# Attention into a gated feed-forward layer: x's sums on DVE, the gates in two pairs, an earlier w_out unit, and x's first parts in halves

## The chip, the cores and the metric

One core of a Trainium2 chip runs the whole program. Its engines work side by side, each through its own instructions in order: TensorE (PE, matmuls; PEld, its weight loads), VectorE (DVE), ScalarE (ACT), GpSimd (POOL), and SyncE (SP), which here only issues DMAs. The metric is the time of one execution on the device, in microseconds.

## What is computed

Attention with a causal mask and a decay made from f, for 8 batches, 8 heads, 576 positions and 64 columns a head; its output, as a matrix x of 4608 tokens by 512, goes through a feed-forward layer of width 2048:

```python
scores = scale * np.matmul(q, k.transpose(0, 1, 3, 2))
decay = cum[:, :, :, None] - cum[:, :, None, :]      # cum: running sum of log f
scores = np.where(causal, -1000000000.0, scores + decay)
attn = softmax(scores)
x = (attn @ v) as [4608, 512]
h = x @ w_in                                          # [4608, 2048]
sp = np.maximum(h, 0.0) + np.log1p(np.exp(-np.abs(h)))
g = h * erf(sp)
out = g @ w_out                                       # [4608, 512]
```

## The kernel before, in words

**Attention** is a loop over t = 0 to 68, two iterations to a pair of heads. Iteration t makes the scores of t and runs the later steps of t - 1 to t - 5 (exps, normalize, transposes, evacuate, values, store), so that all engines work at once. Between them lie jobs of the next stage: one or two weight jobs an iteration from `todo`, and `start_x`, which loads and splits x for the first visit of the feed-forward layer, at t = 44, 46, 48, 50, 52 and 59 to 63.

**The feed-forward layer** multiplies numbers split in two parts: a rounded high part and a remainder, three matmuls for a product. The 4608 tokens are six pairs of blocks of 384 tokens. A *visit* is one such pair with one half of the width 2048; there are 12 visits (v), the first six with the first half. A visit has four *units* (k = 0 to 3, `HU` = 4), each with 256 columns of the width, so there are 48 units (n). A unit makes, by a scheme of seven products instead of eight (`PRODUCTS`, sums and differences of the blocks of x and w_in), four tiles h of 128 x 384.

`step(n)` interleaves three units by hand: the products of unit n (`product`, line 169, 42 matmuls), the gates of unit n - 1, and the multiplication with w_out of unit n - 2 (`down`, line 230, 36 matmuls "y"). It has seven places i = 0 to 6; at each there is a product, then its reader, then other work, then six y matmuls (none at i = 5). The engines' order is the order in which step() writes the instructions.
- `consume`: the readers of the products. ACT copies products 0 and 2 (sa, line 182; h, line 187); DVE adds up the others (sb line 185, sc line 190, h line 193). Two PSUM banks alternate, so that a product can start only when its bank's last reader is done.
- Gates of unit n - 1: softplus (line 197) and erf (line 200) on ACT, each with its table load; `gate`, e times h, on DVE (line 203), four at i = 1; `halve` splits the result: a cast on ACT (gh, line 212) and a remainder on POOL (gl, line 213), four at i = 2.
- x of the next visit: five tiles t of 128 x 768 are loaded, and from them seven tiles x are made. `x_sum` (lines 107, 109, in the unit k = 2) and `late_sum` (line 129) make sums and differences; `split_x` casts (line 116), `rest_x` subtracts (line 121). `next_x` does this in the visit's last unit, k = 3, and `both_x` of x's tile 3 is in the next visit's first unit. Of a visit's eleven sums and remainders POOL does ten and DVE one; of the seven casts DVE does four and ACT three. Product i reads the x tile `XSLOT[i]` = 0, 5, 1, 4, 6, 2, 3.
- Weights come as 64-bit numbers. A piece is converted by `magnitude` (ACT, line 380), `normal`, `low_bits` (two instructions) and `join` (DVE, lines 383, 388, 390, 395), and split by `parts` (cast line 406, remainder on POOL line 407); pieces of w_in also need sums (line 433). In attention the first half of w_in and unit 0's w_out are made (`early_work`). `late_work` lays the rest into steps 2 to 20 (`moe.work[n, place]`): first w_out for units 1 to 3, which those units wait for, then the second half of all weights, one piece a step, whose parts (lhi, llo) go to DRAM through four buffers of one tag, and are read back from visit 5 on.

Steps 0 and 1 are already laid into attention's last iterations (`moe_products`, t = 64 to 67).

Of the kernel before, what the change touches and what calls it, by code (L numbers as in the profile page):

```python
# [11 lines left out]
F32 = mybir.dt.float32  # L12
# [4 lines left out]
ALU = mybir.AluOpType  # L17
# [5 lines left out]
P = 128  # L23
# [33 lines left out]
NU = FF // (2 * P)  # L57
HU = NU // 2
# [14 lines left out]
class Moe:  # L73
# [27 lines left out]
            src = self.xt_d[2 * half * P:2 * (half + 1) * P, at:at + TB]  # L101
            self.nc.sync.dma_start(out=t[j], in_=src.rearrange("(k p) t -> p k t", p=P))

    def x_sum(self, v, j):
        t, sub = self.t[v], self.nc.gpsimd
        if j == 0:
            sub.tensor_tensor(out=t[4], in0=t[2], in1=t[3], op=ALU.add)
        else:
            sub.tensor_tensor(out=t[2], in0=t[0], in1=t[2], op=ALU.subtract)

    def split_x(self, v, r, cast):

        t = self.t[v]
        x = self.x_tile(v, r)
        self.src[r] = t[{0: 0, 5: 0, 1: 1, 4: 4, 6: 2, 2: 1, 3: 3}[r]]
        cast(out=x[:, 0], in_=self.src[r])  # L116

    def rest_x(self, v, r, eng):

        x = self.x[v, r]  # L120
        eng.tensor_tensor(out=x[:, 1], in0=self.src[r], in1=x[:, 0].bitcast(F32), op=ALU.subtract)  # L121

    def both_x(self, v, r, cast, eng):
        self.split_x(v, r, cast)
        self.rest_x(v, r, eng)

    def late_sum(self, v, j, eng):
        t = self.t[v]
        eng.tensor_tensor(out=t[j], in0=t[4 if j == 0 else 1], in1=t[0], op=ALU.subtract)  # L129
# [135 lines left out]
    def step(self, n):  # L265

        v, k = divmod(n, HU)
        up, gates = n < self.n, 1 <= n <= self.n
        downs = self.down(n - 2) if n >= 2 else iter(())
        after = v + 1 < len(self.visits) and n < self.n  # L270
        if n >= 2 and (n - 1) % HU == HU - 1 and self.visits[(n - 1) // HU][1]:
            for tb in range(4):
                self.want_part((n - 1) // HU, tb)
        if gates:
            self.softplus(n - 1, 0)
            self.softplus(n - 1, 1)
        if after and (n == 2 or v and k == 1):
            self.load_x(v + 1)
        for i in range(7):
            if up:  # L280
                self.product(n, i)
                self.consume(n, i)
            if up and v and k == 0 and i == 0:
                self.both_x(v, 3, self.nc.vector.tensor_copy, self.nc.gpsimd)
            if gates and i == 0:
                for q in (2, 3):
                    self.softplus(n - 1, q)
                for q in range(4):
                    self.erf(n - 1, q)
            if after and i < 2:  # L290
                self.next_x(v + 1, k, i)
            if gates and i == 1:
                for q in range(4):
                    self.gate(n - 1, q)
            if gates and i == 2:
                self.do(n, "abs")
            if up and i == (2 if gates else 5):
                self.nc.scalar.preload_act_table_set(SOFTPLUS)
            if gates and i == 2:
                for q in range(4):  # L300
                    self.halve(n - 1, q)
            if after and i >= 2:
                self.next_x(v + 1, k, i)
            for _ in range(YCUT[i + 1] - YCUT[i]):
                next(downs, None)
            self.do(n, i)
            yield
        for _ in downs:
            pass
        if self.reload:  # L310
            self.reload(n)
# [3 lines left out]
def attention_moe(ctx, tc, q2, k2, vp, f, w_in, w_out, out):  # L315
    nc = tc.nc
# [153 lines left out]

    def late_work():

        pieces = [(a, i) for a in range(1, HU) for i in (2, 3)] + [(a, i) for a in range(HU, NU) for i in (2, 3, 0, 1)]
        load, magnitude, normal, low_bits, join, out_parts, quarter_parts, sums, sum_parts = weight_work(
            pieces, late_buf, nc.scalar.copy)
        for m in range(3):
            load(m)
        steps = {2: [0, 1, 2], 3: [3], 4: [4, 5]}
        steps.update({n: [n + 1] for n in range(5, len(pieces) - 1)})
        places = {1: [(3, 4, 5, 6)], 2: [(2, 3, 3, 4), (4, 5, 5, 6)], 3: [(2, 2, 3, 4), (3, 4, 4, 5), (5, 5, 6, 6)]}  # L480
        for n, ms in steps.items():
            for m, (a, b, c, d) in zip(ms, places[len(ms)]):
                moe.work[n, "abs"].append(lambda m=m: magnitude(m))
                moe.work[n, a].append(lambda m=m: normal(m))
                moe.work[n, b].append(lambda m=m: low_bits(m))
                moe.work[n, c].append(lambda m=m: (join(m), load({0: 3, 1: 4, 2: len(pieces)}.get(m, m + 2))))
                i = pieces[m][1]
                if m < 6:
                    moe.work[n, d].append(lambda m=m: out_parts(m))
                elif i >= 2:  # L490
                    moe.work[n + 1, 3].append(lambda m=m: out_parts(m))
                elif i == 0:
                    moe.work[n + 1, 3].append(lambda m=m: quarter_parts(m, 0))
                else:
                    moe.work[n + 1, 1].append(lambda m=m: sums(m, 0))
                    moe.work[n + 1, 2].append(lambda m=m: sums(m, 1))
                    for f in range(2):
                        moe.work[n + 1, 3 + f].append(lambda m=m, f=f: quarter_parts(m, f))
                    for w, at in enumerate((4, 5, 5, 6)):
                        moe.work[n + 1, at].append(lambda m=m, w=w: sum_parts(m, w))  # L500

    load_weight, todo = early_work()

    def start_x(j):

        if j == 0:
            a = wp.tile([P, 2, 2, TB], F32, name="ta", tag="wo2")
            b = wp.tile([P, 2, 2, TB], F32, name="tb", tag="wo3")
            c = wp.tile([P, 2, TB], F32, name="tc", tag="wo1")
            moe.t[0] = t = [a[:, 0], a[:, 1], b[:, 0], b[:, 1], c]  # L510
            for m, (token, half) in enumerate([(0, 0), (0, 1), (1, 0), (1, 1)]):
                for kd in range(2):
                    nc.sync.dma_start(out=t[m][:, kd], in_=moe.x_block(0, token, 2 * half + kd))
        elif j < 3:
            moe.x_sum(0, j - 1)
        else:
            r = [0, 5, 1, 4, 6, 2, 3][j - 3]
            moe.both_x(0, r, nc.scalar.copy, nc.vector if r in (0, 5) else nc.gpsimd)
            if r in (0, 1):
                moe.late_sum(0, r, nc.vector)  # L520

    moe_pools = ctx.enter_context(ExitStack())
    with ExitStack() as ph:
# [160 lines left out]
        NH = B * H  # L684
# [34 lines left out]
        for t in range(NH + 5):  # L719
# [52 lines left out]
        assert not todo and not pts and not held and not vals  # L772
# [54 lines left out]
```

## Time and profile before

| | us |
|---|---|
| median of 3 runs | 1158.06 (1157.95 to 1159.73) |
| the profiled execution | 1156.83 |
| its span, first to last instruction | 1155.0 |
| first product of unit 0 | 320.02 |
| last product's unit (47) starts | 1116.97 |

The mean clock that was granted to TensorE is 0.983 of full speed. In the rows of the profile, a group or a timeline row gives the line of the kernel, the engine, the operation, and output <- inputs by the program's tile names; in square brackets stands how long the engine was idle before it, and whose end released it. A row of the windows view gives a stretch, its length, then the busy time of PE, PEld, DVE, ACT and POOL with the number of instructions, the granted clock, and the share and rate of the DMA engines.

### The profile page before, as it was taken

The page shows a single profiled execution, that of the slowest core. Times are in us where ns is not written, and L with a number is a line of the kernel's source. Part 1 is how long each engine was busy: PE and PEld are TensorE (multiplying, and loading weights), DVE is VectorE, ACT ScalarE, POOL GpSimd, SP SyncE. Part 2 cuts the span into 40 slices and gives each one's busy share as a digit, 9 for nine tenths or more (in the row PEclk, how much of TensorE's full clock was granted, in tenths as well). Part 3 has the DMA queues.
Part 4 walks back from the last instruction along what each step waited for, and adds up shares of the span by engine and source line. Part 5 has one row for each costly group of instructions (what it writes and reads, how often), then busy time and mean ns, then how long its engine had stood idle before and what let it go on. Part 6 is the DMA issues. An engine that isn't in the chain of part 4 may idle for free.

```text
span 1155.0 us, 21292 instructions
## 1 busy us (share of the span) xinstructions
PE 1092.3 (95%) x7384; PEld 951.1 (82%) x7384; DVE 800.1 (69%) x1707; ACT 745.7 (65%) x1672; POOL 753.5 (65%) x841
## 2 busy tenths in 40 slices
PE   8999999999997799898998989999999999999997
PEld 7888888878886688787887878888888888888886
DVE  5898999999746666968778595645647484655632
ACT  3888888877865456575575666566655566555652
POOL 3787978798845836858576695755647383755612
PEclk8999999999999799999999999999999999999999
DMA  7777777776414032152433417542221313031022
GB/s 236 237 244 223 262 215 266 264 260 205 131 42 156 19 114 87 47 200 73 142 115 103 151 39 261 225 160 75 70 95 56 110 55 110 15 115 36 23 87 73
DMA packets 74907, 155.83 MB, mean 135 GB/s; under 512 B 7472, under 2 KB 27184, under 8 KB 73776
## 3 DMA queue, kind: packets, MB, share of 16 engines
q1 hardware_dynamic: 74800, 154.47, 40.1%
q8 instruction: 59, 0.97, 0.3%
q14 instruction: 48, 0.39, 0.1%
HBM read 114.44 MB, written 39.99 MB: 134 GB/s over the span
## 4 chain that ended last, share of the span: by engine, by line
PE 64%; POOL 12%; DVE 10%; ACT 6%; issue 4%; DMA 3%; SPq 0%; DVEq 0%; POOLq 0%; ACTq 0%
PE y L230 21%; PE m L169 20%; PE s L585 8%; PE o L666 8%; PE t L639 7%; POOL gl L213 4%; DVE e L203 3%; POOL x L121 3%; POOL t L129 3%; ACT e L200 2%; ACT e L197 2%; ACT L200 1%; DMA wi_d<-lhi 1%; DMA xt_d<-xo 1%; DVE ltop L395 1%
## 5 line engine op out<-in xcount | busy, mean ns | idle before, releaser
L169 PE MATMUL m<-x,wi 128*128 128x384 f32 x2016 | 404.7, 339 | 29.7 <-DVE sc L190 13.1
L169 PEld LDWEIGHTS m<-x,wi 128*128 128x128 f32 x2016 | 361.3, 190 | 63.0 <-DVE h L193 16.9
L230 PE MATMUL y<-wo,gh 128*128 128x512 f32 x1152 | 363.4, 396 | 16.0 <-POOL wo L407 12.4
L213 POOL TENSOR_TENSOR gl<-e,gh 128x384 fp32r<-128x384 f32 x192 | 221.5, 1183 | 236.4 <-ACT gh L212 209.5
L230 PEld LDWEIGHTS y<-wo,gh 128*128 128x128 f32 x1152 | 214.6, 190 | 46.8 <-POOL wo L407 14.1
L230 PE MATMUL y<-wo,gl 128*128 128x512 f32 x576 | 230.9, 401 | 0.0
L203 DVE TENSOR_TENSOR e<-e,h 128x384 f32<-128x384 f32 x192 | 185.9, 1028 | 33.1 <-ACT e L200 28.2
L627 POOL TENSOR_SCALAR pr<-pr,st 128x576 f32<-128x576 f32 (+4 forms) x320 | 164.0, 533 | 50.1 <-DVE st L623 26.0
L617 ACT ACTIVATE pr<-pr,st 128x576 f32<-128x576 f32 (+3 forms) x320 | 176.7, 557 | 8.0 <-DVE st L605 8.0
L121 POOL TENSOR_TENSOR x<-t,x 128x768 fp32r<-128x768 f32 x66 | 135.9, 2076 | 65.1 <-DVE x L116 65.1
L605 DVE CUSTOM_DVE_ANT_0 pr<-s,c 128x576 f32<-128x576 f32 (+3 forms) x320 | 136.5, 486 | 28.3 <-PE s L589 19.5
L197 ACT ACTIVATE e<-h 128x384 f32<-128x384 f32 x192 | 93.3, 520 | 82.4 <-DVE h L193 82.4
L230 PEld LDWEIGHTS y<-wo,gl 128*128 128x128 f32 x576 | 109.3, 190 | 23.0
L185 DVE TENSOR_TENSOR sb<-m,sa 128x384 f32<-128x384 f32 x48 | 26.7, 555 | 146.7 <-PE m L169 112.7
L585 PE MATMUL s<-k,q 64*128 64x320 f32 (+4 forms) x768 | 110.5, 410 | 3.4 <-DVE st L605 3.2
L648 ACT COPY pt<-t 128x512 f32<-128x512 f32 x128 | 73.9, 577 | 55.5 <-PE t L639 53.7
L212 ACT CAST gh<-e 128x384 fp32r<-128x384 f32 x192 | 88.9, 511 | 29.6 <-DVE e L203 28.7
L639 PE MATMUL t<-ident,pr 128*128 128x128 f32 x800 | 104.5, 276 | 3.0 <-ACT pt L648 2.9
L666 PE MATMUL o<-pt,v 128*64 128x128 f32 (+1 forms) x1920 | 103.1, 260 | 3.3 <-DVE xo L675 2.3
L666 PEld LDWEIGHTS o<-pt,v 128*64 128x64 f32 x1920 | 94.2, 138 | 13.4 <-DVE st L605 4.7
L639 PEld LDWEIGHTS t<-ident,pr 128*128 128x128 f32 x800 | 87.4, 141 | 15.2 <-issue 11.6
L585 PEld LDWEIGHTS s<-k,q 64*128 64x128 f32 x768 | 73.1, 188 | 32.1 <-issue 17.6
(96 smaller groups left out, 1206.2 us busy)
## 6 DMA issues: line engine op xcount, KB each, us to landing
v<-in_vp_dram SPq DMA_DIRECT2D x32, 576.0 KB, 6.9
c<-cum_d SPq DMA_DIRECT2D x62, 288.0 KB, 5.8
t<-xt_d SPq DMA_DIRECT2D x44, 384.0 KB, 5.5
q<-in_q_dram SPq DMA_DIRECT2D x32, 320.0 KB, 3.5
k<-in_k_dram SPq DMA_DIRECT2D x32, 288.0 KB, 3.9
xt_d<-xo SPq DMA_DIRECT2D x32, 288.0 KB, 6.2
part_d<-yo SPq DMA_DIRECT2D x36, 256.0 KB, 2.7
yo<-part_d SPq DMA_DIRECT2D x36, 256.0 KB, 3.0
```

The source lines that it names most:

```text
L121: eng.tensor_tensor(out=x[:, 1], in0=self.src[r], in1=x[:, 0].bitcast(F32), op=ALU.subtract)
L169: nc.tensor.matmul(out=ps, lhsT=w[:, wp, ws], rhs=x[:, xp, kd], start=first and kd == 0 and j == 0, stop=kd == 1 and j == 2 and i in (1, 2 ...
L197: self.nc.scalar.activation(out=e, in_=self.h[n, q], func=AF.Softplus)
L203: self.nc.vector.tensor_mul(self.e[n, q], self.e[n, q], self.h.pop((n, q)))
L213: nc.gpsimd.tensor_tensor(out=gl, in0=e, in1=gh.bitcast(F32), op=ALU.subtract)
L230: yield nc.tensor.matmul(out=y[tb], lhsT=g[:, cs], rhs=w[:, f, wp], start=first, stop=last)
L585: nc.tensor.matmul(out=s[j][:, at:at + k1 - k0], lhsT=q[h, PAD + START[i]:PAD + END[i]], rhs=k[h, k0:k1], start=i > 0, stop=i not in (0, 3))
L605: nc.vector.tensor_tensor_reduce(out=to[:, ::-1] if j else to, in0=score, in1=decay_, scale=-0.125, scalar=BIG, op0=ALU.add, op1=ALU.min, ...
L617: nc.scalar.activation(out=seg, in_=seg, func=AF.Exp, bias=st[:, 0, j, m:m + 1], scale=-1.0, accum_out=st[:, 1, j, m:m + 1])
L627: nc.gpsimd.tensor_scalar(out=seg, in0=seg, scalar1=st[:, 2, j, m:m + 1], scalar2=1.0, op0=ALU.mult, op1=ALU.mult)
L639: nc.tensor.transpose(out=b[:, n * P:(n + 1) * P], in_=probs[t][:, at:at + P], identity=ident)
L666: nc.tensor.matmul(out=o[h, to:to + width], lhsT=v[:, ch, h], rhs=pt[:, at[j]:at[j] + width], start=n == 0, stop=n == len(parts) - 1, skip ...
```

## The change

1. `x_sum`, `late_sum` and `rest_x` of all visits but the first run on DVE; `split_x` always casts on ACT. They are laid out anew: `next_x` does x0, x5, x1, x4 and the cast of x6 in the unit k = 3, and the new `last_x` does the rest of x6, x2 and x3 at i = 0, 1, 2 of the next visit's first unit.
2. Gates 0 and 1 stay at i = 1, gates 2 and 3 go to i = 3; halve of 0 and 1 stays at i = 2, of 2 and 3 goes to i = 3.
3. `late_work` starts one step earlier: unit 1's w_out is converted in step 1, in attention's tail, with buffers in the places of w_out 2 and 3; its parts come at i = 1 of step 2. Units 2 and 3 follow in steps 2 to 4. For the second half of the weights a visit's pieces are two of w_in in its unit k = 1, one of w_out in k = 2 and one in the next visit's k = 0, none in k = 3 (where the remaining parts of a w_out piece still come, at i = 2). The seven parts of w_in lie in k = 2.
4. x of the first visit is loaded from t = 24 on; its sums and its tiles 0 and 5 are made in halves of 384 columns, one job every second iteration up to t = 58. The other five tiles stay at t = 59 to 63.

```diff
-    def x_sum(self, v, j):
-        t, sub = self.t[v], self.nc.gpsimd
+    def x_sum(self, v, j, eng, kd=slice(0, 2)):
+        t = self.t[v]
...
     def next_x(self, v, k, i):
...
         if i == 1:
-            self.split_x(v, 0, dve)
-            self.rest_x(v, 0, pool)
-            self.late_sum(v, 0, pool)
+            self.split_x(v, 0)
+        elif i == 2:
+            self.rest_x(v, 0, dve)
+            self.late_sum(v, 0, dve)
+        elif i == 3:
+            self.split_x(v, 5)
+            self.split_x(v, 1)
         elif i == 4:
-            self.split_x(v, 5, dve)
-            self.both_x(v, 1, act, pool)
-            self.late_sum(v, 1, pool)
+            self.rest_x(v, 5, dve)
         elif i == 5:
-            self.rest_x(v, 5, self.nc.vector)
-            self.both_x(v, 6, act, pool)
+            self.rest_x(v, 1, dve)
+            self.late_sum(v, 1, dve)
+            self.split_x(v, 4)
         elif i == 6:
-            self.both_x(v, 4, dve, pool)
-            self.both_x(v, 2, act, pool)
+            self.rest_x(v, 4, dve)
+            self.split_x(v, 6)
+
+    def last_x(self, v, i):
+
+        dve = self.nc.vector
+        if i == 0:
+            self.split_x(v, 2)
+            self.rest_x(v, 6, dve)
+        elif i == 1:
+            self.rest_x(v, 2, dve)
+            self.split_x(v, 3)
+        elif i == 2:
+            self.rest_x(v, 3, dve)
...
             if up and v and k == 0 and i == 0:
-                self.both_x(v, 3, self.nc.vector.tensor_copy, self.nc.gpsimd)
+                self.last_x(v, 0)
...
-            if gates and i == 1:
-                for q in range(4):
+            if gates and i in (1, 3):
+                for q in (i - 1, i):
                     self.gate(n - 1, q)
+            if up and v and k == 0 and i in (1, 2):
+                self.last_x(v, i)
...
-            if gates and i == 2:
-                for q in range(4):
+            if gates and i in (2, 3):
+                for q in (2 * i - 4, 2 * i - 3):
                     self.halve(n - 1, q)
...
     def late_work():
 
-        pieces = [(a, i) for a in range(1, HU) for i in (2, 3)] + [(a, i) for a in range(HU, NU) for i in (2, 3, 0, 1)]
+        pieces = [(a, i) for a in range(1, HU) for i in (2, 3)] + [(a, i) for a in range(HU, NU) for i in range(4)]
...
+        first, second, only = (2, 2, 4), (4, 5, 6), (4, 5, 6)
+        plan = [(1, first, 2, 1), (1, second, 2, 1), (2, first, 3, 2), (2, second, 3, 3), (3, (5, 5, 6), 4, 2), (4, first, 4, 5)]
+        for n in range(5, 5 + HU * HU, HU):
+            plan += [(n, first, n + 1, 3), (n, second, n + 1, 3), (n + 1, only, n + 2, 2), (n + 3, only, n + 4, 2)]
+        for m, (n, (a, b, c), to, at) in enumerate(plan):
+            moe.work[n, "abs"].append(lambda m=m: magnitude(m))
+            moe.work[n, a].append(lambda m=m: normal(m))
+            moe.work[n, b].append(lambda m=m: low_bits(m))
+            moe.work[n, c].append(lambda m=m: (join(m), load(m + 2) if m > 1 else None))
+            i = pieces[m][1]
+            if i >= 2:
+                moe.work[to, at].append(lambda m=m: out_parts(m))
+            elif i == 0:
+                moe.work[to, at].append(lambda m=m: quarter_parts(m, 0))
+            else:
+                moe.work[to, 2].append(lambda m=m: (sums(m, 0), sums(m, 1)))
+                for f in range(2):
+                    moe.work[to, at + f].append(lambda m=m, f=f: quarter_parts(m, f))
+                for w in range(4):
+                    moe.work[to, at + (3 + w) // 2].append(lambda m=m, w=w: sum_parts(m, w))
...
+    def first_x():
+
+        work = [lambda j=j: load_first(j) for j in range(4)]
+        halves = [slice(kd, kd + 1) for kd in range(2)]
+        for j in range(2):
+            work += [lambda kd=kd, j=j: moe.x_sum(0, j, nc.gpsimd, kd) for kd in halves]
+        for r in (0, 5):
+            work += [lambda kd=kd, r=r: moe.split_x(0, r, kd) for kd in halves]
+            work += [lambda kd=kd, r=r: moe.rest_x(0, r, nc.vector, kd) for kd in halves]
+            if r == 0:
+                work += [lambda kd=kd: moe.late_sum(0, 0, nc.vector, kd) for kd in halves]
+        return work
...
-            if NH - 20 <= t < NH - 10 and t % 2 == 0:
-                start_x((t - NH + 20) // 2)
+            if t >= 24 and t % 2 == 0 and x_work:
+                x_work.pop(0)()
             if NH - 5 <= t < NH:
-                start_x(t - NH + 10)
+                start_x(t - NH + 5)
+            if t == NH:
+                load_late(0)
+                load_late(1)
```

More of the change, by code (lines that the diff above doesn't have):

```diff
@@ L102, in load_x, with split_x, rest_x, late_sum @@
             self.nc.sync.dma_start(out=t[j], in_=src.rearrange("(k p) t -> p k t", p=P))
-    def x_sum(self, v, j):
-        t, sub = self.t[v], self.nc.gpsimd
+    def x_sum(self, v, j, eng, kd=slice(0, 2)):
+        t = self.t[v]
         if j == 0:
-            sub.tensor_tensor(out=t[4], in0=t[2], in1=t[3], op=ALU.add)
+            eng.tensor_tensor(out=t[4][:, kd], in0=t[2][:, kd], in1=t[3][:, kd], op=ALU.add)
         else:
-            sub.tensor_tensor(out=t[2], in0=t[0], in1=t[2], op=ALU.subtract)
-    def split_x(self, v, r, cast):
+            eng.tensor_tensor(out=t[2][:, kd], in0=t[0][:, kd], in1=t[2][:, kd], op=ALU.subtract)
+    def split_x(self, v, r, kd=slice(0, 2)):
         t = self.t[v]
[L114 to L118, printed above, removed]
-        x = self.x[v, r]
[L121 to L127, printed above, removed]
+        if (v, r) not in self.x:
+            self.x_tile(v, r)
+            self.src[r] = t[{0: 0, 5: 0, 1: 1, 4: 4, 6: 2, 2: 1, 3: 3}[r]]
+        self.nc.scalar.copy(out=self.x[v, r][:, 0, kd], in_=self.src[r][:, kd])
+    def rest_x(self, v, r, eng, kd=slice(0, 2)):
+        x = self.x[v, r]
+        eng.tensor_tensor(out=x[:, 1, kd], in0=self.src[r][:, kd], in1=x[:, 0, kd].bitcast(F32), op=ALU.subtract)
+    def late_sum(self, v, j, eng, kd=slice(0, 2)):
         t = self.t[v]
-        eng.tensor_tensor(out=t[j], in0=t[4 if j == 0 else 1], in1=t[0], op=ALU.subtract)
+        eng.tensor_tensor(out=t[j][:, kd], in0=t[4 if j == 0 else 1][:, kd], in1=t[0][:, kd], op=ALU.subtract)
     def next_x(self, v, k, i):
-        act, dve, pool = self.nc.scalar.copy, self.nc.vector.tensor_copy, self.nc.gpsimd
+        dve = self.nc.vector
         if k == 2 and i in ((4, 5) if v == 1 else (0, 1)):
-            self.x_sum(v, i - (4 if v == 1 else 0))
+            self.x_sum(v, i - (4 if v == 1 else 0), dve)
         if k != HU - 1:
@@ L447, in late_buf @@
     def late_buf(kind, m, shape, dt=F32):
-        if kind == "raw" and m == 2:
-            kind = "tt"
+        if m < 2 and kind in ("raw", "top"):
+            if m == 0:
+                shared[kind] = wp.tile([P, 2, shape[1]], dt, name=f"tail_{kind}", tag={"raw": "wo3", "top": "wo2"}[kind])
+            return shared[kind][:, m]
         tag, bufs = {"raw": ("raw", 2), "top": ("top", 3), "tt": ("tt", 1), "hi": ("ws", 4), "lo": ("ws", 4)}[kind]
         return moe.eb.tile(shape, dt, name=f"l{kind}{m}", tag=tag, bufs=bufs)
+    shared = {}
     def early_work():
@@ L471, in late_work @@
     def late_work():
-        pieces = [(a, i) for a in range(1, HU) for i in (2, 3)] + [(a, i) for a in range(HU, NU) for i in (2, 3, 0, 1)]
+        pieces = [(a, i) for a in range(1, HU) for i in (2, 3)] + [(a, i) for a in range(HU, NU) for i in range(4)]
         load, magnitude, normal, low_bits, join, out_parts, quarter_parts, sums, sum_parts = weight_work(
             pieces, late_buf, nc.scalar.copy)
-        for m in range(3):
-            load(m)
-        steps = {2: [0, 1, 2], 3: [3], 4: [4, 5]}
@@ L479, in late_work @@
[L479 to L500, printed above, removed]
@@ L502, in attention_moe, with load_first @@
+        return load
     load_weight, todo = early_work()
-    def start_x(j):
+    load_late = late_work()
+    def load_first(j):
         if j == 0:
@@ L509, in start_x @@
             c = wp.tile([P, 2, TB], F32, name="tc", tag="wo1")
[L510 to L520, printed above, removed]
+            moe.t[0] = [a[:, 0], a[:, 1], b[:, 0], b[:, 1], c]
+        token, half = divmod(j, 2)
+        for kd in range(2):
+            nc.sync.dma_start(out=moe.t[0][j][:, kd], in_=moe.x_block(0, token, 2 * half + kd))
+    def first_x():
[9 more added lines that the diff above has]
+        return work
+    x_work = first_x()
+    def start_x(j):
+        r = [1, 4, 6, 2, 3][j]
+        moe.split_x(0, r)
+        moe.rest_x(0, r, nc.gpsimd)
+        if r == 1:
+            moe.late_sum(0, 1, nc.vector)
     moe_pools = ctx.enter_context(ExitStack())
@@ L771, in attention_moe @@
                 moe.ps_m = moe_pools.enter_context(tc.tile_pool(name="ps_m", bufs=1, space=PSUM, side="right"))
-        assert not todo and not pts and not held and not vals
+        assert not todo and not x_work and not pts and not held and not vals
     moe.eb = ctx.enter_context(tc.tile_pool(name="eb", bufs=1))
     moe.ps_y = ctx.enter_context(tc.tile_pool(name="ps_y", bufs=1, space=PSUM))
-    late_work()
+    load_late(2)
+    load_late(3)
     last = HU * NPAIR
```

1 line of the change is left out of this document (added).

## The prediction

> **What bounds the kernel now.** I read the page first, then cut the span into stages with the windows view, then asked who ended TensorE's waits in each stage (its timeline), then the costs of the instructions that the change moves.
>
> ```profile
> span 1155.0 us, 21292 instructions
> PE 1092.3 (95%) x7384; PEld 951.1 (82%) x7384; DVE 800.1 (69%) x1707; ACT 745.7 (65%) x1672; POOL 753.5 (65%) x841
> 436.87:452.51 15.64, 15.64 (x80) 14.07 (x79) 9.64 (x16) 9.92 (x18) 9.09 (x7) 1.00 0.27 85
> 366.51:436.87 70.36, 54.52 (x236) 46.68 (x234) 43.72 (x53) 35.35 (x64) 47.23 (x31) 0.85 0.19 66
> 452.51:469.38 16.87, 15.80 (x79) 13.87 (x77) 13.11 (x14) 10.65 (x18) 12.12 (x9) 1.00 0.19 68
> 469.38:744.53 275.15, 257.29 (x1248) 226.85 (x1249) 202.54 (x248) 176.24 (x327) 194.16 (x139) 0.99 0.38 133
> 744.53:808.63 64.10, 63.10 (x313) 56.09 (x312) 34.27 (x43) 39.31 (x70) 37.63 (x27) 1.00 0.37 141
> 808.63:1067.82 259.19, 251.37 (x1250) 224.56 (x1248) 154.70 (x189) 151.28 (x268) 150.57 (x105) 1.00 0.23 74
> 1067.82:1085.69 17.87, 15.90 (x79) 13.94 (x78) 14.07 (x13) 10.58 (x19) 15.44 (x10) 1.00 0.00 0
> ```
>
> TensorE is the bound, and a unit without a wait takes 15.64 us (third row: PE busy for all of it). So I count each stage as its excess over 15.64 us a unit; the cuts lie at the first product of a unit, every 42 matmuls of line 169.
> - Units 3 to 5 (366.51 on): 70.36 - 3 x 15.64 = 23.4 us, with the clock at 0.85.
> - Unit 7 and the four visits after it, which still split weights: 1.2 + (275.15 - 16 x 15.64 = 24.9) = 26.1 us.
> - Visit 6: 1.5 us. Visits 7 to 10: 259.19 - 250.24 = 8.95, 2.24 a visit; visit 11's first unit 2.23. Together 12.7 us.
>
> Attention before that has its own rate. The first two rows hold four of its iterations each (from t = 44 and t = 49), the third two near its end (t = 60, 61):
>
> ```profile
> 219.68:238.60 18.92, 18.92 (x226) 15.76 (x223) 17.09 (x68) 15.18 (x49) 14.80 (x26) 1.00 0.97 337
> 243.28:266.20 22.92, 20.44 (x226) 16.52 (x223) 22.62 (x71) 16.48 (x51) 20.38 (x35) 1.00 0.63 212
> 299.51:310.56 11.05, 9.96 (x115) 8.44 (x112) 7.78 (x33) 9.06 (x27) 8.93 (x13) 1.00 0.26 83
> ```
>
> Undisturbed it is 18.92 us. Where start_x casts and subtracts whole tiles it is 22.92: 4.0 us lost, with DVE busy for 22.62. The third row loses 11.05 - 18.92 / 2 = 1.6.
>
> What ends TensorE's waits:
>
> ```profile
> 372.28 0.80 PE L230 MATMUL y<-wo,gh 128*128 128x512 f32 x1 [4.33 <-POOL wo L407]
> 402.66 0.80 PE L230 MATMUL y<-wo,gh 128*128 128x512 f32 x1 [5.88 <-POOL wo L407]
> 511.01 1.31 PE L169 MATMUL m<-x,wi 128*128 128x384 f32 x6 [1.03 <-ACT sa L182]
> 543.50 1.33 PE L169 MATMUL m<-x,wi 128*128 128x384 f32 x6 [2.02 <-DVE h L193]
> 822.93 2.35 PE L169 MATMUL m<-x,wi 128*128 128x384 f32 x12 [1.95 <-DVE sc L190]
> 436.87 1.21 PE L169 MATMUL m<-x,wi 128*128 128x384 f32 x6
> 439.30 1.21 PE L169 MATMUL m<-x,wi 128*128 128x384 f32 x6
> ```
>
> In units 3 and 4 it is w_out's parts that come late. At a visit's start it is a PSUM bank whose reader on DVE (h, sc) is late. The last two rows give the pitch, 2.43 us from a product to the next; the second half of a bank's pair must be read within one or two of these. Why DVE is late:
>
> ```profile
> 846.64 1.96 DVE L203 TENSOR_TENSOR e<-e,h 128x384 f32<-128x384 f32 x4 [0.21 <-ACT e L200]
> 862.46 6.09 DVE L203 TENSOR_TENSOR e<-e,h 128x384 f32<-128x384 f32 x4
> 850.69 0.56 DVE L190 TENSOR_TENSOR sc<-m,sb 128x384 f32<-128x384 f32 x1 [2.08 <-PE m L169]
> 850.64 3.93 POOL L213 TENSOR_TENSOR gl<-e,gh 128x384 fp32r<-128x384 f32 x4 [7.95 <-ACT gh L212]
> L121 POOL TENSOR_TENSOR x<-t,x 128x768 fp32r<-128x768 f32 x66 | 135.9, 2076 | 65.1 <-DVE x L116 65.1
> L121 DVE TENSOR_TENSOR x<-t,x 128x768 fp32r<-128x768 f32 x11 | 24.8, 2252 | 0.0
> L129 DVE TENSOR_TENSOR ta<-ta 128x768 f32<-128x768 f32 x1 | 1.0, 957 | 2.6 <-POOL x L121 2.6
> L116 ACT CAST x<-t 128x768 fp32r<-128x768 f32 x33 | 26.5, 834 | 69.4 <-POOL t L129 69.3
> ```
>
> Four gates take 1.96 us in a unit where POOL is idle, 6.09 in a visit's last unit, where POOL subtracts x tiles. Two-input work on DVE and POOL takes turns: the same 768 columns cost DVE 0.96 us alone and 2.25 beside POOL.
>
> **The change part by part.** *Second half and visit 6 (12.7 us).* Before, POOL did ten of a visit's eleven sums and remainders at some 2 us each. Now DVE does all eleven, at 0.96 us if POOL rests, and hands its four casts to ACT at 0.83. In the last unit DVE then holds six sums (5.7 us), four gates (2.0) and five bank readers of 0.55 (2.7): 10.4 of 15.64. POOL holds only the four gl of 1.0. I laid it out by hand: gates 0 and 1 meet an idle POOL; gates 2 and 3 take turns with two gl and end near 11.5 us; h of product 4, behind them, ends near 12, and is wanted at 13.2. Casts of x5 and x1 follow on ACT until 13.6, so x5's subtraction ends near 14.4, h of product 5 at 14.9 (wanted at 15.6), two sums, h of product 6 at 17.1 (wanted at 18.1). In the next unit x2 is ready at 7 us (wanted at 12.2) and x3 at 8.1 (13.2). Nothing is late: -12.7 us. What hides the sums is the slack of some 0.7 to 1.2 us in each of these; if it is gone, about 0.8 us a visit comes back, -8 at worst.
>
> *Units 2 to 5 (23.4 us).* Unit 1's w_out is now split in units 1 and 2, units 2's and 3's one unit ahead of use, so both waits above go, and with them the clock:
>
> ```profile
> 370.86:381.10 10.24, 7.46 (x18) 5.87 (x19) 2.82 (x5) 5.70 (x11) 7.02 (x5) 0.50 0.00 1
> 544.94:548.35 3.41, 3.41 (x11) 2.95 (x10) 2.16 (x4) 3.38 (x6) 3.19 (x2) 0.50 0.19 77
> 358.23 0.69 DVE L383 SCALAR_TENSOR_TENSOR ltop<-ltop,lraw 128x512 f32<-128x512 f32 x1 [1.20 <-ACT ltop L380]
> 360.50 0.68 DVE L395 SCALAR_TENSOR_TENSOR ltop<-ltop,lraw 128x512 int32<-128x512 int32 x1
> L407 POOL TENSOR_TENSOR wo<-ltop,wo 128x512 fp32r<-128x512 f32 x6 | 8.2, 1373 | 2.0 <-ACT wo L406 2.0
> ```
>
> What is next late is DVE. A piece costs it some 2.5 us (first and last of four instructions). Unit 2 has two pieces and two sums (5.0 + 1.9) beside gates and readers (4.7) and POOL's four gl and two w_out remainders (6.7), which it must take turns with: about 0.9 us over. Unit 3 has one piece and six sums; h of product 6 stands behind two of them and the piece, 2 us too late, which unit 4 pays, with 0.4 more of its own; units 3 and 5 about 0.7 each. After: 0.9 + 0.7 + 2.4 + 0.7 = 4.7, so -18.7. Bounds after: 1 (all hidden) to 12 (half remains).
>
> The second row here is a clock row: a wait of 2.02 us at 543.5 is followed by 3.41 us at half clock. The Trainium skill (TensorE: Matmul & The Clock Gate, section Why this matters for your kernels) asks only that gaps stay under about 3 us; by it, gaps like those that I leave would cost no clock. Here the measurement differs, so up to 1.7 us may follow a gap of 2; I keep that in the upper bound.
>
> *Attention's tail.* Steps 0 and 1 run between attention's last pieces:
>
> ```profile
> 343.05 1.28 ACT L298 ACT_TABLE_LOAD   x1
> 344.34 1.75 ACT L212 CAST gh<-e 128x384 fp32r<-128x384 f32 x4
> 346.00 0.58 ACT L648 COPY pt<-t 128x512 f32<-128x512 f32 x1
> 346.26 0.68 DVE L646 COPY pt<-t 128x512 f32<-128x512 f32 x1
> 347.77 1.66 PE L666 MATMUL o<-pt,v 128*64 128x128 f32 x32
> ```
>
> Two magnitudes now stand ahead of the table load on ACT (1.2 us), and gates 2 and 3 with their casts stand ahead of the last pt copies on DVE and ACT. Gate 3, taking turns with two gl from 346.1, ends near 348.9, its cast at 349.4, pt near 350; the o matmuls wait for pt until then instead of 347.77. That is +2.3 us; bounds 0 (gates win their turns) and +3.5.
>
> *First x parts in halves.* The same instructions, spread over iterations 24 to 58: the 4.0 us go, but DVE, at 17.1 of 18.92 us already, gets six half-size steps of some 0.5 us, and POOL four of 1.0; I let 1.0 stay. -3.0, bounds -4 and 0. The 1.6 us near the end are untouched. x's loads may wait on SP for a store of the same rows, but q, k and c behind them are asked for two iterations ahead. The two new weight loads at t = 64 wait on SP for x's last remainder; only a store two iterations on stands behind them. Both at nothing; if that cover is gone, a late load shows as a gap of PE of one transfer.
>
> *First half (26.1 us).* The two w_in pieces of a unit now meet in the visit's third unit: seven parts instead of six. The row that decides:
>
> ```profile
> 509.35 0.41 ACT L406 CAST lhi<-ltt 128x256 fp32r<-128x256 f32 x1
> 510.50 0.46 ACT L182 COPY sa<-m 128x384 f32<-128x384 f32 x1
> L407 POOL TENSOR_TENSOR llo<-ltt,lhi 128x256 fp32r<-128x256 f32 x16 | 11.8, 735 | 12.5 <-DMA wi_d<-llo 7.9 <-ACT lhi L406 2.3 <-ACT e L197 2.2
> ```
>
> The sixth part is cast at 509.35, 4.4 us into the next unit (504.95), because parts go through four buffers and each waits for POOL and a store; sa stands behind it on ACT, and TensorE waits 1.03 (row at 511.01). A seventh part puts sa about 1 us later: 2.0 us of wait, and now in the visit's last unit. There ACT is then 5 us late with the erfs, the cast of x0 and the table, so gates 2 and 3 meet gl 0 and 1 and end at about 16.5: h of product 4 is 1.7 us late; x5's subtraction pushes h of product 5 another 0.7; small ones 0.5. 4.9 a visit, four visits 19.6. The second unit, with two w_in pieces on DVE, 0.6 in three visits; the piece in the first unit 0.2 in four. After: 22.2, so -3.9. Bounds: 3 after (the part chain ends before sa) to 34 (the turns go on into the next unit, with a half clock).
>
> Sum: -12.7 - 18.7 + 2.3 - 3.0 - 3.9 = -36.0. The profiled execution took 1156.83, so 1120.8; the median of the runs is 1.23 above it, and on that scale I forecast 1122.0 us.
>
> **The rivals.**
> 1. *The part chain is no trouble*: without the second unit's copies in between, its seventh part ends before sa is due. For it: six of the seven parts waited for POOL or a store, and the stores share SP with fewer others now. Against: the wait is there at six parts already. First half 4 instead of 22: 1104.
> 2. *w_out is in time, but units 2 to 4 stay bound by DVE*: x's sums and the pieces pile up, half of 18.7 comes back: 1131.
> 3. *Slower: DVE becomes the bound in a visit's last unit.* If each sum there costs the 2.25 us of the row for DVE beside POOL, and a gate 1.0, the unit needs 6 x 2.25 + 4 + 2.7 = 20.2, 4.6 too much, in eleven visits 51; with some 1.8 more in the first and the third unit of the four loaded visits (14) that is 65 for the 38.8 won: +26, and with -19.4 from the rest +7, 1165. It decides from a mean of about 2.1 us a sum. Against it: POOL's four gl hold 4 us a unit, so six sums can't wait over 0.7 each on average, 1.6 to 1.7 in all. The Trainium skill (SBUF — State Buffer, section Who interferes with whom) says of a DVE instruction with two SBUF inputs that it contends with POOL's reads, whole instructions at a time; by it too a sum waits for at most the gl in hand. Row 862.46 agrees.
>
> **How the numbers follow.** The forecast's own case, 1112 to 1130, gets 0.55; rival 1 0.27; rival 2 0.14; rival 3 0.04. A measurement of this kernel tells about 0.2% (2.3 us) from no change. Slower is rival 3, 0.04; same is the far end of rival 2, 0.02; faster 0.94. The range reaches down to rival 1's value and up past rival 2's by its clock losses: 1104 to 1138.
>
> **What would show it.** Right: visits 7 to 11 at 62.6 us each with no wait of a product at 13 us; no wait of y for wo in units 3 to 5 and clock 1.00 there; o late by some 2 us at 348; a wait for sa in units 7, 11, 15 and 19 and one for h behind it; attention's four iterations from t = 49 under 20 us. Wrong: sums on DVE of over 1.6 us on average, a first half without waits for sa (rival 1), or waits for h all through units 2 to 4 (rival 2).

## The result, and the profile after

The kernel after took 1123.35 us (median of 4 runs, 1122.33 to 1124.44), the kernel before 1158.89 us beside it (1157.95 to 1160.21): a ratio of 0.9693 [0.9676, 0.971]. The forecast was 1122.0. The profiled execution after took 1124.44 us, and 1156.83 before.

The totals of the page after:

```profile
span 1122.7 us, 21302 instructions
PE 1084.4 (97%) x7384; PEld 945.6 (84%) x7384; DVE 781.1 (70%) x1776; ACT 782.1 (70%) x1718; POOL 533.2 (47%) x733
```

POOL gave up 220 us of its 753.5. DVE took its sums over and was still busy for 19 us *less* than before: it handed 44 casts (51.7 us) to ACT, its gates, which took turns with POOL's sums, fell from 185.9 to 144.4 us, and the four steps of the 22 late weight pieces from 95.6 to 72.0. The windows of the kernel after, cut at the same instructions as before (iterations 49 to 52 and 60 to 61 of attention; then units 0 and 1, unit 2, units 3 to 5, units 6 to 23, units 24 to 46):

```profile
242.82:262.96 20.14, 19.71 (x227) 16.14 (x223) 19.97 (x72) 15.82 (x50) 17.98 (x33) 1.00 0.75 237
296.12:307.35 11.23, 9.96 (x115) 8.43 (x111) 7.95 (x33) 9.06 (x27) 9.75 (x15) 1.00 0.24 82
316.81:351.06 34.25, 29.41 (x247) 27.31 (x244) 17.80 (x36) 20.08 (x42) 13.25 (x20) 0.90 0.19 66
351.06:369.32 18.26, 16.04 (x79) 13.84 (x79) 9.92 (x19) 10.79 (x19) 6.78 (x6) 1.00 0.48 163
369.32:421.11 51.79, 49.15 (x234) 43.20 (x235) 40.44 (x56) 38.02 (x66) 21.44 (x16) 0.97 0.26 91
421.11:724.51 303.40, 287.41 (x1406) 251.69 (x1406) 207.38 (x301) 213.43 (x384) 121.67 (x108) 1.00 0.38 129
724.51:1084.23 359.72, 359.72 (x1796) 323.32 (x1795) 209.16 (x301) 234.17 (x409) 103.86 (x92) 1.00 0.26 87
```

The last row is 23 units of 15.64 us with PE busy throughout: nothing is left to win there with this work on TensorE. The rows of before that answer to rows three, four and six:

```profile
320.02:350.50 30.48, 27.80 (x246) 25.78 (x243) 11.74 (x29) 18.74 (x40) 12.60 (x20) 0.94 0.12 40
350.50:366.51 16.01, 15.89 (x79) 14.04 (x79) 11.49 (x21) 11.06 (x19) 3.73 (x3) 1.00 0.70 257
436.87:744.53 307.66, 288.73 (x1405) 254.79 (x1404) 225.29 (x277) 196.81 (x363) 215.36 (x153) 0.99 0.36 127
```

So the span's 32.3 us come from these stages:

| term of the forecast | forecast, us | measured, us |
|---|---|---|
| units 24 to 46 (second half, visit 6) | -12.7 | -12.7 (372.44 to 359.72) |
| units 2 to 5 | -18.7 | -16.3 (unit 2 +2.3, units 3 to 5 -18.6) |
| units 0 and 1 (attention's tail) | +2.3 | +3.8 |
| first x parts in halves (iteration 20 to unit 0) | -3.0 | -1.2 (213.90 to 212.69) |
| units 6 to 23 (first half) | -3.9 | -4.3 |
| start to iteration 20; unit 47 and after | 0 | -2.0; +0.4 |

The change does not touch the start, up to iteration 20; over the profiled executions here it took 102.5 to 106.1 us, whatever the kernel. The medians lie 35.5 us apart and not 32.3: the execution profiled after is the slowest of its four.

What ends TensorE's waits after (its timeline, from unit 1 to unit 7):

```profile
346.74 2.66 PE L697 MATMUL o<-pt,v 128*64 128x128 f32 x32 [2.16 <-DVE xo L706]
352.98 0.70 PE L242 MATMUL y<-wo,gh 128*128 128x512 f32 x2 [0.71 <-PE m L181]
369.32 1.33 PE L181 MATMUL m<-x,wi 128*128 128x384 f32 x6 [1.51 <-DVE h L205]
388.38 0.50 PE L242 MATMUL y<-wo,gh 128*128 128x512 f32 x1 [1.17 <-POOL wo L421]
390.59 1.50 PE L181 MATMUL m<-x,wi 128*128 128x384 f32 x6 [1.48 <-DVE h L205]
443.91 1.33 PE L181 MATMUL m<-x,wi 128*128 128x384 f32 x6 [2.01 <-ACT sa L194]
454.01 1.34 PE L181 MATMUL m<-x,wi 128*128 128x384 f32 x6 [1.34 <-DVE h L205]
```

Of the waits for w_out, the longest of which were 4.33 and 5.88 us, one of 1.17 is left. The waits for sa and, behind it, for h stand in unit 7 (from 436.87 on) and alike in units 11, 15 and 19, each a visit's last unit, as forecast; these four units took 4.43 to 5.12 us too long, against 4.9.

### The profile page after: what moved, and what is told of

The parts are those of the page before. It is cut to its first block, busy times and chain, and to the rows that moved or that the text cites. A ratio compares the mean times of both kernels' runs of the same rounds, so it can differ in the third digit from the quotient of the medians.

```text
span 1122.7 us, 21302 instructions
## 1 busy us (share of the span) xinstructions
PE 1084.4 (97%) x7384; PEld 945.6 (84%) x7384; DVE 781.1 (70%) x1776; ACT 782.1 (70%) x1718; POOL 533.2 (47%) x733
## 4 chain that ended last, share of the span: by engine, by line
PE 67%; issue 17%; POOL 8%; DMA 3%; DVE 3%; ACT 1%; SPq 0%; POOLq 0%; DVEq 0%; ACTq 0%
PE y L242 22%; PE m L181 20%; PE s L616 8%; PE o L697 8%; PE t L670 7%; POOL gl L225 5%; POOL llo L421 2%; DMA wi_d<-llo 1%; DVE pr L636 1%; DMA xt_d<-xo 1%; PE s L620 1%; POOL wo L421 1%; PE idle L735 0%; DMA lraw<-in_w_out_dram 0%; ACT e L212 0%
## 5 line engine op out<-in xcount | busy, mean ns | idle before, releaser
L225 POOL TENSOR_TENSOR gl<-e,gh 128x384 fp32r<-128x384 f32 x192 | 224.4, 1197 | 489.8 <-ACT gh L224 476.2
L242 PE MATMUL y<-wo,gh 128*128 128x512 f32 x1152 | 359.2, 393 | 1.9 <-POOL wo L421 1.2
L242 PEld LDWEIGHTS y<-wo,gh 128*128 128x128 f32 x1152 | 212.7, 188 | 30.5 <-POOL wo L421 1.6
L215 DVE TENSOR_TENSOR e<-e,h 128x384 f32<-128x384 f32 x192 | 144.4, 793 | 28.2 <-ACT e L212 28.2
L224 ACT CAST gh<-e 128x384 fp32r<-128x384 f32 x192 | 92.0, 512 | 59.6 <-DVE e L215 59.0
L122 DVE TENSOR_TENSOR x<-t,x 128x768 fp32r<-128x768 f32 x77 | 80.3, 1054 | 18.9 <-ACT x L117 18.9
```

The source lines that it names most:

```text
L215: self.nc.vector.tensor_mul(self.e[n, q], self.e[n, q], self.h.pop((n, q)))
L224: nc.scalar.copy(out=gh, in_=e)
L225: nc.gpsimd.tensor_tensor(out=gl, in0=e, in1=gh.bitcast(F32), op=ALU.subtract)
L242: yield nc.tensor.matmul(out=y[tb], lhsT=g[:, cs], rhs=w[:, f, wp], start=first, stop=last)
```

## The experiments

The theory: what is left in units 6 to 23 is the chain of a w_in piece's seven parts, through ACT, POOL and a store, which holds ACT's queue and so sa; the early w_out unit removed the waits for w_out; the sums pay on DVE because a sum costs it about 1 us there; the gates by twos are what delays attention's tail. The rivals: in units 6 to 23 DVE is short, with or without the chain; w_out's old place would have done, once the sums have left POOL; the new places of the sums matter, not the engine; halves of x give the whole gain ahead of unit 0. All kernels below are the kernel after with one edit, the last two with two and three. The kernel before took 1157.32 us beside the first four and 1157.56 beside the last three, against 1158.89 beside the kernel after, so a difference of less than 1.6 us from the kernel after tells nothing.

**A part in one buffer.** A part took two of the four buffers of its tag, so the third part's cast waits for the first one's store. Here the two halves of a part share one:

```diff
-                hi, lo = (buf(x, m, [P, width], F32R) for x in ("hi", "lo"))
+                both = buf("hi", m, [P, 2, width], F32R)
+                hi, lo = both[:, 0], both[:, 1]
```

(for parts of w_in; w_out's stay in two).

> The changed kernel, but the high part and the remainder of a w_in part share one of the four store buffers, so that four parts instead of two are under way. My theory: the 21.9 us that units 6 to 20 still lose come from the seven-part chain, which holds sa back on ACT in units 7, 11, 15 and 19. The seventh part is then cast some 2.5 us earlier, sa comes in time, the wait for sa (2.0 to 2.7 us in each) goes and most of the later waits for h with it: 10 to 16 us faster than the changed kernel, about 1109. Rival (DVE, with its sums and its turns with POOL, sets these units): the wait for sa goes, but h is as late as before: 0 to 3 us faster.

Measured: 1111.28 us (1111.02 to 1112.83), ratio 0.9598 [0.957, 0.9625]; 12.1 us less than after. ACT's timeline of the kernel after, in unit 7 (from 436.87):

```profile
442.25 0.41 ACT L420 CAST lhi<-ltt 128x256 fp32r<-128x256 f32 x1 [0.79 <-DMA wi_d<-lhi]
443.40 0.46 ACT L194 COPY sa<-m 128x384 f32<-128x384 f32 x1
```

The same of this kernel (unit 7 from 434.19):

```profile
437.63 0.41 ACT L424 CAST lhi<-ltt 128x256 fp32r<-128x256 f32 x1 [0.73 <-DMA wi_d<-lhi]
438.78 0.46 ACT L194 COPY sa<-m 128x384 f32<-128x384 f32 x1
```

sa came 6.5 us into the unit, and 5.5 before the change; now 4.6, and no product waits for it. Units 6 to 23, by the windows view of this kernel:

```profile
418.46:713.13 294.67, 287.39 (x1405) 251.70 (x1405) 207.18 (x301) 212.59 (x384) 122.90 (x108) 1.00 0.39 132
```

DVE's and ACT's work is the same to 1 us, and 8.7 us of the 21.9 above 18 x 15.64 are gone: these were waits, not a shortage of DVE. The wait for h of product 4, which I had expected to go with the other, stayed, as the rival had it, at 1.31 to 1.34 us in units 7, 11, 15 and 19, and each of these still takes 2.49 to 2.72 us too long. Another 2.7 us of the span lie ahead of unit 6, 1.5 of them in unit 4, where the half clock of the kernel after did not come; the edit does not touch that, so its own worth is nearer to 9 than to 12, and just under the 10 to 16 that I had expected.

**All gates at i = 1 again,** with their halves at i = 2: only the second part of the change undone.

```diff
-            if gates and i in (1, 3):
-                for q in (i - 1, i):
+            if gates and i == 1:
+                for q in range(4):
...
-            if gates and i in (2, 3):
-                for q in (2 * i - 4, 2 * i - 3):
+            if gates and i == 2:
+                for q in range(4):
```

> The changed kernel with all four gates back at i = 1 and all four halves at i = 2. My theory: the second pair of gates, in turns with gl, is what makes attention's last pt copies late (o waits 2.2 us in unit 1) and h of product 4 late in units 7, 11, 15 and 19 (1.3 us each); without the pairs both waits go and nothing else comes late, since x's sums no longer lie on POOL: 6 to 10 us faster than the changed kernel, about 1115. Rival (the pairs are needed, so that DVE reads the products in time between x's sums): waits for sc or h at the start of visits come back, 5 us or more slower.

Measured: 1115.08 us (1114.37 to 1116.22), 0.9632 [0.9608, 0.9656]; 8.3 less than after, as expected. Its windows (units 0 and 1, unit 2, units 6 to 23, units 24 to 46):

```profile
317.20:347.74 30.54, 27.86 (x247) 25.78 (x243) 15.64 (x35) 19.35 (x41) 13.04 (x20) 0.94 0.22 74
347.74:366.41 18.67, 16.15 (x79) 13.95 (x78) 14.11 (x21) 11.22 (x20) 7.96 (x6) 1.00 0.45 159
416.27:714.48 298.21, 287.26 (x1405) 254.82 (x1404) 194.33 (x300) 210.46 (x384) 116.21 (x108) 0.99 0.38 130
714.48:1074.20 359.72, 359.72 (x1795) 323.32 (x1794) 181.12 (x301) 230.72 (x408) 94.29 (x92) 1.00 0.26 87
```

Units 0 and 1 are back at 30.5: without the gates by twos the 3.8 us lost there are gone. Units 6 to 23 win 5.2: the wait for h of product 4 is gone from units 7, 11, 15 and 19, while sa is still waited for there, for 1.56 to 2.60 us, and a wait of 1.04 or 1.05 for h comes back in units 8 and 16. Units 24 to 46 lose nothing, and DVE spends 28 us less there. The groups of the gates and of gl in this kernel, then gl in the kernel after (its gates stand in the next experiment: 793 ns each):

```profile
L215 DVE TENSOR_TENSOR e<-e,h 128x384 f32<-128x384 f32 x192 | 96.4, 564 | 27.6 <-ACT e L212 27.6
L225 POOL TENSOR_TENSOR gl<-e,gh 128x384 fp32r<-128x384 f32 x192 | 204.9, 1098 | 495.9 <-ACT gh L224 483.1 <-issue 12.7
L225 POOL TENSOR_TENSOR gl<-e,gh 128x384 fp32r<-128x384 f32 x192 | 224.4, 1197 | 489.8 <-ACT gh L224 476.2 <-issue 13.6
```

Two gates that run at i = 3 take turns with the gl of the first two; four gates at i = 1 run while POOL rests. Of the change's parts, this one alone was a loss.

**The sums on POOL, at their new places:** `dve = self.nc.vector` becomes `self.nc.gpsimd` in `next_x` and `last_x`.

> The changed kernel with the sums and remainders of x (all visits but the first) on POOL again, in the new places, casts still on ACT. My theory: the second half gained because these 2 us operations left POOL, where the gates and gl must take turns with them; the excess of visits 7 to 11 comes back, 2 us a visit or more, and more in the first half: 15 to 40 us slower than the changed kernel, 1138 to 1163. Rival (the new places and the gates in pairs did it, the engine did not matter): within 4 us of the changed kernel.

Measured: 1184.8 us (1181.43 to 1186.25), 1.0229 [1.0199, 1.0259]: 61 us more than after, half as much again as the upper end of what was expected, and slower than before the change. Two groups of this kernel's instructions by line (busy us, mean ns of one, then the idle time before them):

```profile
L215 DVE TENSOR_TENSOR e<-e,h 128x384 f32<-128x384 f32 x192 | 178.9, 972 | 78.9 <-POOL x L122 58.8 <-ACT e L212 19.8
L122 POOL TENSOR_TENSOR x<-t,x 128x768 fp32r<-128x768 f32 x77 | 143.1, 1876 | 2.1 <-ACT x L117 2.1
```

The same groups of the kernel after:

```profile
L215 DVE TENSOR_TENSOR e<-e,h 128x384 f32<-128x384 f32 x192 | 144.4, 793 | 28.2 <-ACT e L212 28.2
L122 DVE TENSOR_TENSOR x<-t,x 128x768 fp32r<-128x768 f32 x77 | 80.3, 1054 | 18.9 <-ACT x L117 18.9
```

The same subtraction costs POOL 1.88 us and DVE 1.05, and the gates, by the releaser that the first row names, idle 58.8 us behind POOL. I had counted only POOL's queue, not what waits for it. Units 24 to 46 took 388.36 us, 28.6 more than in the kernel after and 15.9 more than before the change; units 6 to 23 took 26.4 more than after, units 3 to 5 9.6. So these places need DVE. Sums on DVE at their old places were not run, so what the places alone are worth stays open.

**First x parts whole,** at t = 44 to 52 as before:

```diff
-        for j in range(2):
-            work += [lambda kd=kd, j=j: moe.x_sum(0, j, nc.gpsimd, kd) for kd in halves]
+        work += [lambda j=j: moe.x_sum(0, j, nc.gpsimd) for j in range(2)]
...
-            if t >= 24 and t % 2 == 0 and x_work:
+            if NH - 20 <= t < NH - 10 and t % 2 == 0:
                 x_work.pop(0)()
```

(and tiles 0 and 5 whole in the same way).

> The changed kernel with x of the first visit loaded at t = 44 and its sums and tiles 0 and 5 made whole at t = 46 to 52, as before the change. My theory: attention's four iterations from t = 49 take 4 us more again and the rest is unchanged: 3.2 us slower than the changed kernel, about 1126.5, with unit 0 at 320.0 instead of 316.8. Rival (unit 0 starts earlier for another reason, such as the order of the loads on SP): no difference.

Measured: 1123.62 us (1122.1 to 1124.69), 0.9704 [0.9678, 0.9729], the time of the kernel after. I had expected 3.2 more. Its windows, iteration 20 to unit 0 and units 0 to 2:

```profile
104.41:318.29 213.88, 210.31 (x2447) 174.90 (x2443) 196.11 (x728) 175.44 (x542) 180.48 (x331) 1.00 0.70 225
318.29:368.14 49.85, 42.78 (x324) 38.22 (x321) 27.82 (x55) 30.87 (x61) 20.57 (x26) 1.00 0.30 105
```

Attention's four iterations from t = 49 took 22.91 again, as expected. Up to unit 0 it took 213.88, as before the change (213.90) and 1.2 us more than after. Units 0 to 2 took 49.85 against 52.51 after, and the clock was 1.00 in them where it was 0.90 after. So the halves win 1.2 us, and in the profiled execution a clock loss of the kernel after covers that; by the times the halves cannot be told from nothing.

**The w_out units late:** w_out for units 1 to 3 in steps 2 to 4, with the old plan, buffers and loads.

```diff
-        plan = [(1, first, 2, 1), (1, second, 2, 1), (2, first, 3, 2), (2, second, 3, 3), (3, (5, 5, 6), 4, 2), (4, first, 4, 5)]
+        plan = [(2, (2, 2, 3), 2, 4), (2, (3, 4, 4), 2, 5), (2, (5, 5, 6), 2, 6), (3, (3, 4, 5), 3, 6), (4, (2, 3, 3), 4, 4),
+                (4, (4, 5, 5), 4, 6)]
```

> The changed kernel with w_out of units 1 to 3 converted in steps 2 to 4 again, at the places of before, the rest as changed. My theory: the early unit is what took away the waits of y for wo in units 3 and 4; they come back with their half clock, while unit 1 loses its wait for o and its 2 us: 10 to 16 us slower than the changed kernel, 1133 to 1139. Rival (units 2 to 5 gained because x's sums left POOL, which the w_out remainders need): within 4 us of the changed kernel.

Measured: 1131.62 us (1129.06 to 1132.68), 0.9777 [0.9745, 0.9809]; 8.3 more than after, where 10 to 16 were expected. Units 0 and 1, and units 2 to 5:

```profile
314.20:345.96 31.76, 27.84 (x246) 25.78 (x243) 12.22 (x29) 18.89 (x40) 12.62 (x20) 0.95 0.11 38
345.96:428.05 82.09, 69.99 (x313) 59.94 (x313) 58.37 (x81) 49.34 (x87) 29.74 (x22) 0.92 0.31 107
```

Units 2 to 5 took 86.4 us before, 82.1 here, 70.05 after: 12.0 of the 16.3 won there are the early unit, 4.3 remain for the rest of the change, the sums on DVE among it. Of the 12.0, 5.1 are the clock: 13.7 us at half clock here, 3.4 in the kernel after, and each costs half its length. Units 0 and 1 take 2.5 less than in the kernel after. Without the gates by twos they took 3.7 less, and the loss there was 3.8 in all, so the early unit and the gates make it together and their shares do not add. The waits for w_out come back at only 0.9 to 1.3 us; a wait of 5.0 for h comes beside them. TensorE's timeline, in units 2 and 4:

```profile
367.13 2.29 PE L181 MATMUL m<-x,wi 128*128 128x384 f32 x6 [5.00 <-DVE h L205]
391.07 0.49 PE L242 MATMUL y<-wo,gh 128*128 128x512 f32 x1 [1.08 <-ACT wo L420]
```

DVE's timeline of this kernel ahead of that h:

```profile
362.12 0.96 DVE L107 TENSOR_TENSOR t<-t,t 128x768 f32<-128x768 f32 x1 [3.44 <-DMA t<-xt_d]
...
366.53 0.55 DVE L205 TENSOR_TENSOR h<-m,sb 128x384 f32<-128x384 f32 x1
```

x's sum, now on DVE, stands there for 3.44 us until x's load has landed; the piece's last steps and h stand behind it.

**One buffer a part and all gates at i = 1**, the first two edits together.

> Both edits at once: w_in parts that share a store buffer, and the gates in one go. My theory: the two remove different waits (sa by the buffers, o and h by the gates), so their gains of 12.1 and 8.3 us add up: 1101 to 1105. Rival (both work on the same stretch of units 7, 11, 15 and 19, and overlap there): 1107 to 1110.

Measured: 1103.21 us (1102.53 to 1104.16), 0.9535 [0.9506, 0.9564]. The two gains add up (12.1 + 8.3 = 20.4; measured 20.1), so they are two separate costs. Units 6 to 23 took 287.98 us, where the least possible is 281.5. Of the waits over half a microsecond those for h in units 8, 12, 16 and 20, of 0.70 to 1.03 us, and one of 0.55 for sa in unit 15 are left there.

**And the second early piece moved** out of the tail into step 2, where it still makes its use:

```diff
-            moe.work[n, a].append(lambda m=m: normal(m))
-            moe.work[n, b].append(lambda m=m: low_bits(m))
+            moe.work[n, 5 if m == 1 else a].append(lambda m=m: normal(m))
+            moe.work[(2, 0) if m == 1 else (n, b)].append(lambda m=m: low_bits(m))
```

(its join too at (2, 0)).

> As the run with both edits, and the second piece of unit 1's w_out has its low bits and join in step 2 at i = 0 instead of step 1. My theory: y of unit 2 waits 1.3 us for a PSUM bank, because the last xo copies of attention stand on DVE behind that piece; with part of it moved behind the copies the wait goes, 1 to 3 us faster than the run with both edits (the half clock after it may go too). Rival (y waits for gl or for wo, not for the bank): no difference, or slower if w_out is late for unit 3.

Measured: 1101.83 us (1100.27 to 1104.44), 0.953 [0.9493, 0.9567]: the fastest here, 21.5 us below the kernel after, though the last 1.4 lie within the spread of the runs. In its trace unit 2's y matmuls no longer wait (1.67 us in the kernel above). Unit 2 of the kernel above, then of this one:

```profile
345.03:363.90 18.87, 16.16 (x79) 13.96 (x78) 14.45 (x21) 11.34 (x20) 7.99 (x7) 1.00 0.45 157
345.03:362.34 17.31, 16.05 (x79) 13.84 (x79) 12.00 (x21) 10.54 (x19) 7.00 (x7) 1.00 0.51 172
```

In the kernel after it took 18.26.

## Why the prediction was right, and where not

**Right: the second half.** The hand layout of a visit's last unit held. DVE's timeline in unit 35 (from 896.55):

```profile
905.56 2.35 DVE L215 TENSOR_TENSOR e<-e,h 128x384 f32<-128x384 f32 x2
907.84 0.54 DVE L205 TENSOR_TENSOR h<-m,sc 128x384 f32<-128x384 f32 x1
909.22 1.36 DVE L122 TENSOR_TENSOR x<-t,x 128x768 fp32r<-128x768 f32 x1 [0.85 <-ACT x L117]
910.51 0.55 DVE L205 TENSOR_TENSOR h<-m,sb 128x384 f32<-128x384 f32 x1
912.83 0.55 DVE L205 TENSOR_TENSOR h<-m,sb 128x384 f32<-128x384 f32 x1
```

Gates 2 and 3 end 11.4 us into the unit (forecast 11.5), h of product 4 at 11.8 (12), x5 at 14.0 (14.4), the next h at 14.5 (14.9) and 16.8 (17.1), each ahead of its need. Rival 3 needed a mean of 2.1 us a sum; the row above has 1.05.

**Right: the first half.** "A seventh part puts sa about 1 us later": 1.0. Its wait of 2.0 was 2.01 in unit 7 and up to 2.7 in the others, h of product 4 waited 1.34 where 1.7 was said. Gates 2 and 3 of unit 7 were to end at about 16.5 us and ended at 16.6 (450.87 and 2.62 us more). h of product 5, which was to wait 0.7 more, did not wait that long. The excess left in units 6 to 23 is 21.9 against 22.2. The wait for sa refutes rival 1's reason that the chain would end in time, and the experiment with one buffer a part shows that the buffers of the chain caused this wait: 8.7 of the 21.9. The wait for h needs the gates by twos as well: it stays with one buffer a part, goes with the gates at i = 1, and with both edits these four units are 0 to 1.11 us too long.

**Right in kind, too small: units 0 to 2.** "That is +2.3 us" for the o matmuls: the wait was 2.16, but the matmuls behind it ran at half clock. The windows of the kernel after at the three places in units 0 to 5 where that was so:

```profile
336.95:340.36 3.41, 3.41 (x19) 2.97 (x21) 0.03 (x1) 1.11 (x3) 0.00 (x0) 0.50 0.02 5
347.19:350.60 3.41, 3.41 (x32) 3.29 (x29) 2.81 (x5) 0.52 (x1) 0.16 (x1) 0.50 0.00 0
391.56:394.97 3.41, 3.41 (x10) 2.82 (x10) 3.24 (x6) 3.38 (x7) 0.00 (x0) 0.50 0.46 157
```

The first follows the wait of 2.68 us for pt that the kernel before has too. The second adds 1.7 us to the 2.16, which about makes the 3.8; the third adds 1.7 in unit 4. The forecast had kept these 1.7 "in the upper bound" and not in the sum. The failed step of units 2 to 5 is "about 0.9 us over" for unit 2: it lost 2.6, 0.71 of it before its first y, where the last run, with the second early piece moved, has no wait, and 1.51 for h of product 5. DVE's timeline there says why h was late:

```profile
366.58 1.01 DVE L107 TENSOR_TENSOR t<-t,t 128x768 f32<-128x768 f32 x1 [3.04 <-DMA t<-xt_d]
367.52 0.68 DVE L409 SCALAR_TENSOR_TENSOR ltop<-ltop,lraw 128x512 int32<-128x512 int32 x1
368.12 0.68 DVE L397 SCALAR_TENSOR_TENSOR ltop<-ltop,lraw 128x512 f32<-128x512 f32 x1
368.72 0.55 DVE L205 TENSOR_TENSOR h<-m,sb 128x384 f32<-128x384 f32 x1
```

I had added up DVE's work and not the wait that the change brings to it: the first sum of the x that is loaded after attention waits for its load and holds DVE for 3 us, with h behind it. Before, this sum stood on POOL (at 368.30), where no reader of a product stands behind it. It happens once, in unit 2. The forecast's own terms for unit 2 add up to 18.3 us, 2.7 over and not 0.9; that this is near 2.6 is chance, since DVE was busy for only 9.92 us there. "No wait of y for wo" and "clock 1.00" in units 3 to 5 also failed: unit 4 lost 4.75 where 2.4 was forecast: 1.17 for a w_out part, 1.7 by the clock, and 1.48 for unit 3's h of product 6, the one wait of the three that the forecast had, at 2. Units 3 and 5 lost 0.1 and nothing where 0.7 each was forecast. Rival 2's case, half of the 18.7 back, did not come.

**Wrong in size: the halves of x.** "The 4.0 us go ... I let 1.0 stay": three other iterations (t = 37, 38 and 42) lost 1.4 together, 1.2 stayed in t = 51 and 52, and t = 60 and 61 took 0.2 more, so 1.2 was won. DVE, at 17.1 of 18.92 us in four such iterations without x's parts, probably has no room for half-size steps either; no run tested that. The 1.6 us lost near the end before the change stayed (1.8, second row of the windows after).

The errors are +2.4, +1.5, +1.8, -0.4, +0.4 and, by the start's -2.0, they shrink to 3.7 of 36. That the median came within 1.4 us of the forecast is in part luck: the medians lie some 3 us further apart than the two profiled executions, and the start, at nothing in the forecast, gave 2.0.

## What to carry to other kernels

Two engines that take turns are best laid out so that each works while the other rests: sums moved from POOL to DVE made DVE's own gates faster, while gates spread over two places met POOL's work and lost; and what moves to a busier engine brings its waits along, not only its time (here x's load). When an in-order engine stands on a cast that waits for a buffer, look at how many buffers a unit of that work takes before moving anything: a shared buffer won 9 us here and cost nothing. Undo each part of a compound change by itself; here one of the four parts was a loss inside a clear gain, and another could not be measured.

## What the runs showed of the hardware

The half clock comes in stretches of 3.41 us or whole multiples of it, and a wait of about 2 us brings it at one time and not at another. The traces show what separates the two. In each trace the stretches start on one grid of 3.413 us: in the kernel after at 336.95, 347.19 and 391.56, which are 3 and 13 steps apart. The wait of 2.68 us for pt, which ends at 336.89 there, lies whole in one step (333.54 to 336.95), and the next step has half clock. In the kernel with x's first parts whole the same wait ends at 338.36. Its only stretch between unit 0 and unit 47 starts at 511.13; counted back 51 steps from there, a step ends at 337.05 and cuts the wait into 1.4 and 1.3 us, and no half clock follows. The 2.01 us in unit 7 of the kernel after are cut in the same way, at 442.76, into 0.9 and 1.1.

Counted so, from 40 us on up to unit 47, the nine traces hold 2726 steps at full clock. After each of the 27 in which TensorE stood idle for 1.90 us or more, half clock followed; after none with less than 1.71; in between, after two of eight. So, as far as these traces tell, it is the idle time within a step that counts, and 1.7 us more or less between two executions can be the place of a wait in the grid alone. No run here varied one wait by itself. The Trainium skill (TensorE: Matmul & The Clock Gate, section Why this matters for your kernels) asks to keep gaps under about 3 us; the 2.16 us at 346.74 that cost 1.7 more show that this is not enough here.

DVE and POOL, both with two inputs, slow each other in both directions. In units 24 to 46 of the kernel after, two gates at i = 1, with POOL idle, take 1.03 us together; two at i = 3, beside gl, take 1.84 to 2.35. With the gates spread so, a gl takes 1.20 us on average, against 1.10 where all four gates run at i = 1.
